# One list, two orders: 3,498 steps of an attention and MLP kernel rearranged around its loads

## The chip, the cores and the metric

One core of a Trainium2 chip. The metric is the device time of one execution in microseconds (us). Five engines work beside each other, each on its own queue of instructions, strictly in order: TensorE (PE, matmuls), VectorE (DVE), ScalarE (ACT), GpSimd (POOL) and SyncE (SP). Here POOL and SP do little but start transfers, which 16 DMA engines then carry out.

## What is computed

Four batches of 6080 tokens with 256 channels. In each batch a 256 x 256 matrix of scores between channels is made from q and k, and v is multiplied by its softmax; a two-layer MLP with 2048 hidden units follows.

```
qn = q / (norm(q, axis=1) + 1e-06);  kn = k / (norm(k, axis=1) + 1e-06)
s  = kn.transpose(0, 2, 1) @ qn / tau
a  = softmax(s, axis=-1)
x  = (v @ a).reshape(B * N, 256)
out = gelu_tanh(x @ w_in) @ w_out
```

## The kernel before

**Tiling.** Since `v @ a @ w_in` is `v @ (a @ w_in)`, the kernel makes one 256 x 2048 matrix `aw` for each batch. The tokens are cut into 25 blocks numbered 0 to 24: five of 1024 and one of 960 in each of the first three batches (blocks 0-5, 6-11, 12-17), and in the last batch five of 1024 (18-22), one of 512 and one of 448. A block runs through the first layer, the GELU, the second layer and the store of its tokens. Both layers use a seven-product scheme in place of eight, with sums made on DVE and copies on ACT. While the blocks of one batch run, the gram matrix, norms and `aw` of the next batch are made in between. Before block 0 there is a start in which batch 0's own q and k are read; the change does not touch it.

**The list.** Everything after that start is one string, `ORDER`, of 3,498 words. `run` takes the words one by one and issues the instructions of each; no scheduler moves them. A word is a step, an optional index, an optional PSUM bank and a block or a batch: `m5.1@b:2` is the fifth small product of set 1 of block 2 into bank b. So the order in which an engine works is the order of the words that issue something on it. Engines are tied to each other by semaphores only, so a word that stands later in the list may still run earlier than its neighbours on another engine.

The words that matter here:

- `lq.c:b`, `lk.c:b` (`load_one`, line 103): POOL starts a load of chunk c of q or k of batch b, 768 rows, cast to bf16 on the way. There are five buffers of each. The load is held back until the latest first- or second-layer product ahead of it in the list has ended (`GATE`).
- `lv.h:n` (`cast_v`, line 442): POOL copies half h of block n of v to a bf16 buffer in DRAM (`vb`), held back in the same way.
- `lt.h:n` (`load_vt`, line 447): SP starts a transposing load from `vb` into `vT`, of which there are two. Nothing holds it back but its data, its buffer, and what stands ahead of it in SP's queue. That is the stores of finished tokens (`store`, line 757), each of which waits for its transposes on DVE.
- `qsq`, `ksq` (`square_op`, lines 158 and 160): the squares of a chunk of q or k, the k of even chunks on DVE and the others on ACT. `row.c_r:b` (line 205): one row group of the chunk into the gram matrix, on PE. These are the uses of a q or k load.
- `vs:n` (lines 558-561, DVE): sums of the transposed halves of v. `g.u:n` (line 482, PE): a plain first-layer product, which reads both halves. `m1` to `m7` (line 482): the small products. These are the uses of `vT`.
- `e.p_t:0` and `E` (block 0's first layer, on PE and ACT), `G`, `wGq`, `wGr`, `wGx` (GELUs on ACT), `wcq`, `wy5` (copies on ACT, lines 613 and 616), `wap`, `wax` (sums on DVE, lines 618 and 621), `T` (sums on DVE, line 704), `M` (second layer, PE), `c11` to `c22` (transposes into the store tile `ot`, DVE, line 744; there are three tiles).
- `D` (second layer of block 24, PE), `sA`, `sB` (its stores).

```
        after(nc.gpsimd.dma_start(out=vb[: y - x, :], in_=v[b, t0 + x : t0 + y, :]), gate)
...
        nc.sync.dma_start_transpose(out=vt_tile(n)[:, :, x:y], in_=v_bf.pop((n, h))[: y - x, :])
...
            elif what in ("lq", "lk"):
                load_one(n, *a, "qk".index(what[1]), GATE[0])
            elif what == "lv":
                cast_v(n, *a, GATE[0])
            elif what == "lt":
                load_vt(n, *a)
```

Of the kernel before, what the change touches and what calls it, by code (L numbers as in the profile page):

```python
# [948 lines left out]
e.0_0@h:0 aw.3@s:0 ac.3:0 aw.2@a:0 e.1_0@b:0 vp.1@r:0 ac.2:0 E.0_0:0 e.2_0@h:0 aw.4@p:0 E.1_0:0  # L949
e.3_0@b:0 lv.1:1 lk.0:1 E.2_0:0 aw.5@s:0 vc.1_0:0 vc.1_1:0 E.3_0:0 e.3_1@h:0 aw.6@a:0 E.3_1:0  # L950
e.0_1@b:0 E.0_1:0 ac.4:0 e.2_1@h:0 ac.5:0 SW.0:0 aw.7@r:0 pA11:0 e.1_1@b:0 E.2_1:0 ac.7:0 e.5_1@h:0
vp.0@p:1 lq.0:1 E.1_1:0 E.5_1:0 e.4_1@b:0 T1.1:0 pF0:0 pS3:0 e.5_0@h:0 pA12:0 vc.0_1:1 ac.6:0
E.4_1:0 M1.0@s:0 pF1:0 vc.0_0:1 e.4_0@b:0 lt.1:1 pS1:0 E.5_0:0 e.6_1@h:0 lq.1:1 pNA:0 E.4_0:0
E.6_1:0 M1.1@s:0 e.6_0@b:0 e.7_1@h:0 ksq.0:1 pS4:0 T1.0:0 lk.1:1 E.6_0:0 row.0_1@r:1 M5.1@a:0
row.0_0@r:1 m1.1@p:1 g.0@b:1 row.0_2@r:1 E.7_1:0 vs:1 lq.2:1 m5.1@h:1 M5.0@a:0 qsq.0:1 wcq.1:1 G.0:1
m6.1:1 f1.0:1 e.7_0@b:0 wy5.1:1 lk.2:1 wap.1:1 m2.1:1 row.0_5@r:1 row.0_4@r:1 row.0_3@r:1 m7.1:1
pA21:0 f2.0:1 SW.1:0 m3.1:1 E.7_0:0 y5:0 wGq.1:1 wax.1:1 g.8@b:1 row.1_4@r:1 T3.0:0 f3.0:1 lv.0:2
row.1_2@r:1 cq:0 m4.1:1 g.10@h:1 wGr.1:1 row.1_3@r:1 row.1_1@r:1 G.8:1 sp.0@p:1 lv.1:2 pS2:0 T2.0:0
T2.1:0 sa.0:1 M2.1:0 M2.0:0 ksq.1:1 qsq.1:1 g.2@b:1 G.10:1 f1.1:1 c11:0 lk.3:1 M6.0:0 f2.1:1
m1.5@p:1 M6.1:0 m5.5@h:1 ap:0 row.1_0@r:1 wcq.5:1 f3.1:1 G.2:1 wy5.5:1 lq.3:1 m2.5:1 m6.5:1  # L960
row.1_5@r:1 T3.1:0 wap.5:1 gc:1 g.3@b:1 M3.1:0 sp.1@r:1 ksq.2:1 lk.4:1 G.3:1 M7.0:0 m3.5:1 M3.0:0
g.11@b:1 T4.0:0 lt.1:2 qsq.2:1 wGq.5:1 lt.0:2 g.12@h:1 f1.2:1 sa.1:1 f2.2:1 M7.1:0 f3.2:1 c12:0
sp.2@r:1 ax:0 wGx.1:1 m7.5:1 G.11:1 m1.6@s:1 sa.2:1 wax.5:1 T4.1:0 G.12:1 g.4@b:1 row.2_1@r:1 lq.4:1
M4.0:0 T1.0:1 m5.6@h:1 row.3_2@r:1 row.3_4@r:1 qsq.3:1 wcq.6:1 G.4:1 m6.6:1 g.7@b:1 wy5.6:1 M4.1:0
wap.6:1 ksq.3:1 lq.5:1 row.3_5@r:1 T2.0:1 wGx.5:1 G.7:1 m4.5:1 m3.6:1 m2.6:1 m7.6:1 row.2_2@r:1
g.15@b:1 f1.3:1 f2.3:1 wax.6:1 wGq.6:1 wGr.5:1 lv.0:3 f3.3:1 c21:0 row.3_0@r:1 row.2_0@r:1 m4.6:1
G.15:1 sp.3@p:1 row.2_5@r:1 row.2_3@r:1 sa.3:1 vs:2 row.2_4@r:1 qsq.4:1 row.3_1@r:1 m1.1@a:2 g.0@h:2
m5.1@b:2 row.3_3@r:1 wcq.1:2 M1.1@p:1 lk.5:1 G.0:2 wy5.1:2 ksq.4:1 m6.1:2 T1.1:1 m2.1:2 wap.1:2
f1.4:1 g.3@h:2 wGx.6:1 wGr.6:1 m3.1:2 m7.1:2 M5.1@s:1 G.3:2 wax.1:2 f2.4:1 lk.6:1 g.8@h:2 f3.4:1
gc:1 wGq.1:2 T2.1:1 m4.1:2 M5.0@s:1 sp.4@r:1 M1.0@p:1 wGx.1:2 lv.1:3 G.8:2 y5:1 m5.2@b:2 sa.4:1  # L970
m1.2@r:2 c22:0 wGr.1:2 T3.0:1 cq:1 m1.5@a:2 m5.5@h:2 wcq.2:2 M2.1:1 m6.2:2 wcq.5:2 M2.0:1 m2.2:2
m6.5:2 wy5.2:2 wy5.5:2 ksq.5:1 T4.1:1 m2.5:2 wap.2:2 c11:1 wap.5:2 m3.2:2 lq.6:1 m7.2:2 wax.2:2
T4.0:1 M6.1:1 M6.0:1 m3.5:2 m4.2:2 wGq.2:2 qsq.5:1 lv.0:4 wGr.2:2 wGq.5:2 g.11@b:2 ap:1 m7.5:2
wGx.2:2 T3.1:1 wax.5:2 f1.5:1 M7.0:1 m1.6@r:2 M7.1:1 m5.6@h:2 G.11:2 lt.0:3 ax:1 f2.5:1 f3.5:1
m4.5:2 g.4@b:2 wcq.6:2 m6.6:2 wGr.5:2 M3.0:1 wy5.6:2 wGx.5:2 sp.5@a:1 M3.1:1 wap.6:2 sa.5:1 G.4:2
m1.7@a:2 m5.7@b:2 m7.6:2 qsq.6:1 ksq.6:1 M4.0:1 m3.6:2 m2.6:2 wcq.7:2 m6.7:2 wy5.7:2 lt.1:3 wax.6:2
m4.6:2 M4.1:1 wGq.6:2 wGx.6:2 f1.6:1 wap.7:2 lq.7:1 m7.7:2 m3.7:2 m2.7:2 f2.6:1 c12:1 g.12@h:2
wax.7:2 wGr.6:2 m1.1@p:3 wGq.7:2 c21:1 T1.0:2 wGx.7:2 row.5_3@r:1 G.12:2 m4.7:2 g.0@b:3 f3.6:1 vs:3
row.5_2@r:1 row.5_0@r:1 row.5_1@r:1 row.5_5@r:1 row.4_2@r:1 row.4_1@r:1 row.5_4@r:1 row.4_4@r:1
m5.1@h:3 wcq.1:3 m1.2@s:3 wGr.7:2 T1.1:2 row.4_3@r:1 G.0:3 sp.6@a:1 m6.1:3 wy5.1:3 m2.1:3  # L980
row.4_5@r:1 wap.1:3 m5.2@b:3 wcq.2:3 lk.7:1 m6.2:3 row.4_0@r:1 sa.6:1 qsq.7:1 m7.1:3 wy5.2:3
M5.1@a:2 m2.2:3 m3.1:3 wax.1:3 gc:1 m4.1:3 M5.0@a:2 wap.2:3 wGx.1:3 wGq.1:3 wGr.1:3 m1.3@r:3 m3.2:3
T3.0:2 m7.2:3 m5.3@h:3 wax.2:3 c22:1 T2.0:2 y5:2 wcq.3:3 wGq.2:3 M1.0@p:2 M1.1@p:2 m6.3:3 wy5.3:3
m4.2:3 T2.1:2 g.8@b:3 m2.3:3 wap.3:3 cq:2 M2.0:2 M2.1:2 ksq.7:1 lv.1:4 wGr.2:3 m3.3:3 m1.5@s:3
M6.0:2 G.8:3 lt.0:4 wGq.3:3 f1.7:1 T3.1:2 f2.7:1 m7.3:3 m5.5@b:3 c11:2 wcq.5:3 f3.7:1 wGx.2:3
g.4@h:3 wy5.5:3 m6.5:3 wax.3:3 wap.5:3 M6.1:2 G.4:3 ap:2 m4.3:3 wGr.3:3 m2.5:3 wGx.3:3 m3.5:3 m7.5:3
wGq.5:3 m5.6@h:3 T4.0:2 sp.7@r:1 M7.1:2 sa.7:1 m1.6@r:3 wcq.6:3 wax.5:3 M7.0:2 m6.6:3 T4.1:2 m4.5:3
wy5.6:3 pow:1 g.12@b:3 wGx.5:3 wap.6:3 wGr.5:3 m2.6:3 m3.6:3 ax:2 G.12:3 kf:1 lt.1:4 lv.0:5 m7.6:3
m1.7@s:3 M4.0:2 wax.6:3 m5.7@b:3 c22:2 wcq.7:3 wGq.6:3 wy5.7:3 m6.7:3 m4.6:3 wGr.6:3 wGx.6:3 wap.7:3
M4.1:2 g.0@h:4 m7.7:3 row.6_2@r:1 m3.7:3 c21:2 m2.7:3 row.7_3@r:1 G.0:4 m1.1@a:4 wax.7:3 m4.7:3  # L990
M3.1:2 M3.0:2 lq.0:2 lv.1:5 wGq.7:3 T1.0:3 vs:4 m5.1@h:4 wGr.7:3 wcq.1:4 c12:2 wy5.1:4 m1.2@s:4
m6.1:4 row.6_5@r:1 m2.1:4 m5.2@b:4 row.7_2@r:1 wap.1:4 wcq.2:4 T1.1:3 m1.3@p:4 row.6_1@r:1 m6.2:4
wGx.7:3 wy5.2:4 wap.2:4 m3.1:4 row.7_1@r:1 m2.2:4 m7.1:4 row.7_5@r:1 wGq.1:4 row.6_4@r:1 wax.1:4
m3.2:4 m7.2:4 row.6_0@r:1 row.7_0@r:1 row.6_3@r:1 row.7_4@r:1 m5.3@h:4 wcq.3:4 T2.1:3 wGq.2:4
wGx.1:4 m4.1:4 m6.3:4 gc:1 m5.4@b:4 m2.3:4 wy5.3:4 wGr.1:4 M5.0@r:3 wax.2:4 wap.3:4 m1.4@a:4 wy5.4:4
m4.2:4 wGx.2:4 lv.0:6 m3.3:4 m7.3:4 M5.1@r:3 T2.0:3 wcq.4:4 wax.3:4 wGr.2:4 m6.4:4 kr:1 lv.1:6
wGq.3:4 lt.0:5 M1.0@s:3 m4.3:4 M1.1@s:3 wGr.3:4 m2.4:4 y5:3 T4.1:3 cq:3 krp@p:1 wap.4:4 wGx.3:4
T4.0:3 m5.5@h:4 m7.4:4 S.1:1 wy5.5:4 th.1:1 S.0:1 th.0:1 wax.4:4 m3.4:4 M2.1:3 m1.5@p:4 T3.0:3
wcq.5:4 M6.0:3 m4.4:4 m6.5:4 M2.0:3 T3.1:3 lt.1:5 wGx.4:4 wGr.4:4 wGq.4:4 wap.5:4 m1.6@a:4 M6.1:3
dn:1 m3.5:4 m7.5:4 m2.5:4 m5.6@b:4 c11:3 wcq.6:4 ap:3 wGq.5:4 wy5.6:4 m6.6:4 wax.5:4 M7.0:3 rc.2:1  # L1000
wap.6:4 m4.5:4 m2.6:4 lk.0:2 g.8@h:4 rc.1:1 wGr.5:4 wGx.5:4 m7.6:4 m3.6:4 m1.7@p:4 M7.1:3 G.8:4
wax.6:4 M3.0:3 m5.7@h:4 m4.6:4 rc.0:1 ax:3 rc.3:1 wGq.6:4 wcq.7:4 c22:3 wGr.6:4 wy5.7:4 M4.0:3
m6.7:4 wap.7:4 M4.1:3 m2.7:4 lv.0:7 wGx.6:4 lq.1:2 m3.7:4 eT:1 m7.7:4 g.0@b:5 c21:3 wax.7:4 wGq.7:4
T1.1:4 G.0:5 rsum@a:1 aw.1@r:1 m4.7:4 g.4@h:5 vs:5 rs:1 M3.1:3 g.8@b:5 c12:3 G.4:5 wGr.7:4 T1.0:4
ac.1:1 m1.1@a:5 m5.1@h:5 aw.0@p:1 wcq.1:5 G.8:5 M5.1@s:4 aw.4@r:1 m6.1:5 wy5.1:5 wGx.7:4 ac.0:1
m2.1:5 m5.2@b:5 m1.2@p:5 wap.1:5 ac.4:1 M5.0@s:4 T2.1:4 m7.1:5 lk.1:2 m3.1:5 lv.1:7 wcq.2:5 y5:4
wy5.2:5 wGq.1:5 wax.1:5 m6.2:5 T3.1:4 M1.1@r:4 m4.1:5 wGr.1:5 M1.0@r:4 m2.2:5 lt.0:6 cq:4 wGx.1:5
wap.2:5 aw.5@a:1 T3.0:4 m7.2:5 g.12@h:5 m3.2:5 T2.0:4 wax.2:5 ac.5:1 wGq.2:5 lt.1:6 M2.1:4 m1.3@a:5
M2.0:4 m4.2:5 m5.3@b:5 wcq.3:5 wy5.3:5 wGx.2:5 wGr.2:5 G.12:5 T4.1:4 m6.3:5 M6.1:4 M6.0:4 c11:4
ksq.0:2 aw.2@p:1 wap.3:5 m7.3:5 m3.3:5 m2.3:5 ap:4 wax.3:5 M7.0:4 m5.5@h:5 ac.2:1 wGq.3:5 m4.3:5  # L1010
m1.5@p:5 M3.0:4 m5.6@b:5 wy5.5:5 wcq.5:5 M3.1:4 m6.5:5 lv.0:8 qsq.0:2 M7.1:4 wGr.3:5 SW.0:1 T4.0:4
c12:4 m1.6@a:5 wap.5:5 aw.3@r:1 ax:4 ac.3:1 wGx.3:5 wcq.6:5 m7.5:5 m3.5:5 m2.5:5 wGq.5:5 M4.0:4
f1.0:2 wy5.6:5 m6.6:5 wax.5:5 wap.6:5 m1.7@r:5 m5.7@h:5 M4.1:4 m2.6:5 m4.5:5 c21:4 m7.6:5 wcq.7:5
m3.6:5 wGx.5:5 wy5.7:5 m6.7:5 wax.6:5 wGr.5:5 aw.6@s:1 wap.7:5 aw.7@p:1 wGq.6:5 m4.6:5 m2.7:5 T1.0:5
m3.7:5 m7.7:5 ac.7:1 wGx.6:5 wGr.6:5 wGq.7:5 g.0@b:6 wax.7:5 ac.6:1 G.0:6 M1.1@a:5 lq.2:2 m1.1@p:6
m4.7:5 lk.2:2 T1.1:5 M5.0@s:5 g.8@h:6 vs:6 lt.0:7 M5.1@s:5 m5.1@b:6 wcq.1:6 wGr.7:5 wGx.7:5 m6.1:6
G.8:6 m1.2@r:6 M1.0@a:5 SW.1:1 wy5.1:6 y5:5 cq:5 lt.1:7 m5.2@h:6 wap.1:6 m2.1:6 m7.1:6 T2.0:5
wax.1:6 m3.1:6 M2.1:5 wcq.2:6 wy5.2:6 m2.2:6 m6.2:6 wGq.1:6 m4.1:6 wap.2:6 M6.0:5 m3.2:6 wGr.1:6
m5.5@b:6 T2.1:5 T3.0:5 m1.5@p:6 M2.0:5 m7.2:6 wGx.1:6 wGq.2:6 wy5.5:6 g.3@h:6 M6.1:5 wcq.5:6 c11:5
# [260 lines left out]
```

## Time and profile before

| | us |
|---|---|
| runs | 687.57, 690.52, 697.32 |
| median of them | 690.52 |
| the profiled execution | 687.86 |
| its span, first to last instruction | 686.1 |
| first matmul of the list begins | 37.91 |
| last matmul ends | 681.03 |
| PE busy | 665.7 (97%) |
| DVE busy | 629.1 (92%) |
| ACT busy | 621.9 (91%) |

A time in the texts that follow is counted from the start of the span of the profiled execution, unless it is a length. "Busy" counts an instruction from its start to its end; PE's ends are modelled and overlap, so the distance between the starts of two matmuls says more than their lengths do. An "idle before" in square brackets is idle time of an engine ahead of an instruction, with what ended it.

### The profile page before, as it was taken

The numbers are of one execution on the slowest core, as the hardware profiler recorded it, in microseconds if no ns is written. First come the engines' busy times: TensorE is split into PE (matmuls) and PEld (weight loads), VectorE is DVE, ScalarE is ACT, GpSimd is POOL, SyncE is SP. The second block draws the span as 40 slices with busy tenths as digits, with TensorE's granted clock in tenths as the row PEclk, the third lists the DMA queues.
The fourth block names the chain that finished last, engine by engine and source line by source line (L and its number), as shares of the span: only waits on it lengthen the run. The fifth ranks groups of instructions, "written<-read, shape, count | busy, mean of one in ns | idle before, by whom it ended". The sixth has DMA issues, their size and how long they took to land.

```text
span 686.1 us, 10286 instructions
## 1 busy us (share of the span) xinstructions
PE 665.7 (97%) x3584; PEld 337.1 (49%) x3584; DVE 629.1 (92%) x938; ACT 621.9 (91%) x941; POOL 74.2 (11%) x137
## 2 busy tenths in 40 slices
PE   3999999999999999999999999989999999999997
PEld 2854445454445454544444545535444444444566
DVE  3579999999999999999999999979999999999994
ACT  5389999998899999999989999979989999999983
POOL 4321111110001010100010101101000000000001
PEclk9999999999999999999999999999999999999999
DMA  9999897584888987655569998636473543445415
GB/s 240 207 251 158 124 171 114 102 143 74 142 103 118 167 114 98 100 96 93 103 105 142 142 157 138 84 53 108 79 135 62 91 75 61 72 83 90 76 32 89
DMA packets 161508, 78.80 MB, mean 115 GB/s; under 512 B 148512, under 2 KB 152224, under 8 KB 160736
## 3 DMA queue, kind: packets, MB, share of 16 engines
q0 software_dynamic: 14480, 39.72, 36.8%
q1 hardware_dynamic: 145728, 37.14, 31.4%
q10 hardware_dynamic: 1248, 1.28, 0.6%
q8 instruction: 28, 0.46, 0.3%
q14 instruction: 24, 0.20, 0.1%
HBM read 78.91 MB, written 36.57 MB: 168 GB/s over the span
## 4 chain that ended last, share of the span: by engine, by line
PE 85%; DMA 7%; issue 4%; ACT 2%; POOL 1%; DVE 0%; DVEq 0%; POOLq 0%; ACTq 0%
PE p L482 22%; PE r L482 17%; PE rb L482 16%; PE qp L482 12%; PE h L482 10%; PE G L205 4%; DMA qk_g1b<-in_k_dram 3%; PE awp L374 2%; DMA qk_g1a<-in_q_dram 1%; DMA k<-in_k_dram 1%; DMA q<-in_q_dram 1%; ACT g L516 1%; PE e L482 1%; ACT g L637 0%; ACT qp L613 0%
## 5 line engine op out<-in xcount | busy, mean ns | idle before, releaser
L482 PEld LDWEIGHTS <-wcomb 128*128 128x128 bf16 x1408 | 136.5, 98 | 144.5 <-issue 1.7
L482 PE MATMUL p<-t,wcomb 128*128 128x512 bf16 (+2 forms) x576 | 142.8, 373 | 0.1
L482 PE MATMUL r<-g,wcomb 128*128 128x512 bf16 (+2 forms) x576 | 141.8, 373 | 0.0
L626 ACT ACTIVATE g<-qp 128x1024 bf16<-128x1024 f32 (+1 forms) x130 | 132.0, 1022 | 6.1 <-PE qp L482 5.9
L482 PEld LDWEIGHTS <-aw 128*128 128x128 bf16 x872 | 84.8, 98 | 94.8 <-issue 6.3
L704 DVE TENSOR_TENSOR t<-g,t 128x2048 bf16<-128x2048 bf16 (+2 forms) x96 | 112.8, 1182 | 0.0
L482 PE MATMUL rb<-tv,sw 128*128 128x512 bf16 (+3 forms) x288 | 101.4, 366 | 0.1
L618 DVE TENSOR_TENSOR qp<-rb,yw 128x512 f32<-128x512 f32 (+2 forms) x137 | 93.1, 686 | 8.7 <-ACT yw L616 4.8
L621 DVE TENSOR_TENSOR xw<-rb,yw 128x512 f32<-128x512 f32 (+2 forms) x137 | 92.6, 676 | 7.1 <-ACT g L637 3.4
L516 ACT ACTIVATE g<-h 128x1024 bf16<-128x1024 f32 (+1 forms) x92 | 94.1, 1032 | 1.8 <-PE h L482 1.4
L482 PE MATMUL h<-vT,aw 128*128 128x512 bf16 (+2 forms) x376 | 95.0, 377 | 0.6 <-ACT g L516 0.5
L616 ACT ACTIVATE yw<-qp 128x512 f32<-128x512 f32 (+2 forms) x137 | 80.8, 601 | 5.8 <-PE qp L482 4.1
L613 ACT ACTIVATE qp<-rb 128x512 f32<-128x512 f32 (+2 forms) x137 | 80.8, 595 | 4.7 <-PE rb L482 3.4
L637 ACT ACTIVATE g<-xw 128x512 bf16<-128x512 f32 (+1 forms) x130 | 82.1, 635 | 2.2 <-DVE xw L621 2.2
L482 PEld LDWEIGHTS <-sw 128*128 128x128 bf16 x576 | 56.2, 98 | 56.6 <-issue 0.6
L637 ACT ACTIVATE g<-rb 128x512 bf16<-128x512 f32 (+1 forms) x130 | 77.6, 602 | 1.9 <-PE rb L482 1.8
L704 DVE TENSOR_TENSOR t<-g 128x2048 bf16<-128x2048 bf16 (+2 forms) x48 | 56.5, 1181 | 0.7 <-ACT g L626 0.4
L704 DVE TENSOR_TENSOR g<-g,g 128x2048 bf16<-128x2048 bf16 (+2 forms) x48 | 56.6, 1183 | 0.0
L442 POOL DMA_DIRECT2D vb<-in_v_dram x45 | 22.5, 501 | 312.1 <-PE rb L482 199.4
L482 PE MATMUL rb<-tv,aw 128*128 128x512 bf16 (+3 forms) x144 | 50.9, 366 | 2.5 <-DVE xw L621 2.5
L482 PE MATMUL rb<-vT,aw 128*128 128x512 bf16 (+3 forms) x144 | 51.3, 366 | 0.0
L482 PE MATMUL qp<-vT,aw 128*128 128x512 bf16 (+3 forms) x144 | 51.3, 366 | 0.0
(143 smaller groups left out, 815.2 us busy)
## 6 DMA issues: line engine op xcount, KB each, us to landing
out_dram<-ot SPq DMA_DIRECT2D x160, 128.0 KB, 3.1
vb<-in_v_dram POOLq DMA_DIRECT2D x38, 256.0 KB, 4.6
k<-in_k_dram POOLq DMA_DIRECT2D x21, 384.0 KB, 5.6
q<-in_q_dram POOLq DMA_DIRECT2D x21, 384.0 KB, 5.2
out_dram<-ot SPq DMA_DIRECT2D x24, 120.0 KB, 4.0
wst<-in_moe_w_out_dram POOLq DMA_DIRECT2D x2, 1024.0 KB, 10.5
vb<-in_v_dram POOLq DMA_DIRECT2D x6, 240.0 KB, 4.1
qk_f<-in_k_dram ACTq DMA_DIRECT2D x2, 512.0 KB, 6.9
```

The costliest lines, as they stand in the source:

```text
L205: nc.tensor.matmul(G[b][:, jc, :], lhsT=qt[:np_, r, jc * 128 : jc * 128 + 128], rhs=kt[:np_, r, :], start=first and jc == 0, stop=jc == 1, ...
L374: nc.tensor.matmul(ps, lhsT=ET[b][:, jc, ic * 128 : ic * 128 + 128], rhs=win_bf[:, jc, fs * 512 : fs * 512 + 512], start=jc == 0, stop=jc ...
L442: after(nc.gpsimd.dma_start(out=vb[: y - x, :], in_=v[b, t0 + x : t0 + y, :]), gate)
L482: GATE[0] = nc.tensor.matmul(*a, skip_group_check=True, **kw)
L516: nc.scalar.activation(g_half(n, u // 8)[:, u % 8].rearrange("p (t x) -> p t x", t=2), hp[:, :, :hc], AF.Gelu_apprx_tanh)
L613: apart(n, i, 0, "act", nc.scalar.activation(QP[n, i][:, 0, :w], RB[n, i][:, :w], AF.Copy))
L616: apart(n, i, 1, "act", nc.scalar.activation(YW[n, i][:, :w], QP[n, i][:, 1, :w], AF.Copy))
L618: apart(n, i, 1, "dve", nc.vector.tensor_add(QP[n, i][:, 1, :w], RB[n, i][:, :w], YW[n, i][:, :w]))
L621: nc.vector.tensor_add(XW[n, i][:, :w], RB[n, i][:, :w], YW.pop((n, i))[:, :w])
L626: nc.scalar.activation(g[:, k0].rearrange("p (t x) -> p t x", t=2), qp[:, :, :hc], AF.Gelu_apprx_tanh)
L637: nc.scalar.activation(g[:, k0, t], x[:, :w], AF.Gelu_apprx_tanh)
L704: nc.vector.tensor_sub(o, a, b)
```

## The change

Only `ORDER` differs. Both lists hold the same 3,498 words, PSUM banks aside: no step is added or removed, and each engine has the same instructions to do. Nearly all of them stand in another place, and many products go to another bank. The rule behind the new order is that transposing loads of v lie apart from loads of q and k, and that the first use of each load lies some us behind its landing. Cut to the places that are spoken of (the left-out lines differ throughout as well):

```diff
-e.0_0@h:0 aw.3@s:0 ac.3:0 aw.2@a:0 e.1_0@b:0 vp.1@r:0 ac.2:0 E.0_0:0 e.2_0@h:0 aw.4@p:0 E.1_0:0
-e.3_0@b:0 lv.1:1 lk.0:1 E.2_0:0 aw.5@s:0 vc.1_0:0 vc.1_1:0 E.3_0:0 e.3_1@h:0 aw.6@a:0 E.3_1:0
-e.0_1@b:0 E.0_1:0 ac.4:0 e.2_1@h:0 ac.5:0 SW.0:0 aw.7@r:0 pA11:0 e.1_1@b:0 E.2_1:0 ac.7:0 e.5_1@h:0
-vp.0@p:1 lq.0:1 E.1_1:0 E.5_1:0 e.4_1@b:0 T1.1:0 pF0:0 pS3:0 e.5_0@h:0 pA12:0 vc.0_1:1 ac.6:0
-E.4_1:0 M1.0@s:0 pF1:0 vc.0_0:1 e.4_0@b:0 lt.1:1 pS1:0 E.5_0:0 e.6_1@h:0 lq.1:1 pNA:0 E.4_0:0
-E.6_1:0 M1.1@s:0 e.6_0@b:0 e.7_1@h:0 ksq.0:1 pS4:0 T1.0:0 lk.1:1 E.6_0:0 row.0_1@r:1 M5.1@a:0
-row.0_0@r:1 m1.1@p:1 g.0@b:1 row.0_2@r:1 E.7_1:0 vs:1 lq.2:1 m5.1@h:1 M5.0@a:0 qsq.0:1 wcq.1:1 G.0:1
...
-m1.5@p:1 M6.1:0 m5.5@h:1 ap:0 row.1_0@r:1 wcq.5:1 f3.1:1 G.2:1 wy5.5:1 lq.3:1 m2.5:1 m6.5:1
...
-m4.6:14 lk.7:3 wGq.7:14 wax.7:14 m1.2@a:15 row.5_4@s:3 T1.0:14 g.0@b:15 m4.7:14 wGr.6:14 G.0:15
...
-m6.2:15 gc:3 wy5.1:15 wy5.2:15 wGx.7:14 wap.1:15 ksq.7:3 M5.1@p:14 m7.1:15 wap.2:15 wax.1:15
...
-m3.3:24 wGq.3:24 wGx.2:24 wGx.1:24 m7.3:24 D.2_1@r:24 D.2_0@s:24 D.6_0@s:24 D.0_0@s:24 c21:23 c22:23
...
-c11:24 c21:24 sB:24 D.4_1@r:24 D.7_1@r:24 D.0_1@r:24 D.3_1@r:24 c22:24 c12:24 sA:24
+e.1_0@h:0 aw.3@s:0 ac.3:0 aw.2@a:0 e.0_0@b:0 ac.2:0 vp.1@r:0 E.1_0:0 vc.1_1:0 vc.1_0:0 e.2_0@h:0
...
+SW.0:0 E.3_1:0 e.2_1@h:0 aw.6@a:0 E.0_1:0 e.1_1@b:0 lv.1:1 E.2_1:0 aw.7@r:0 ac.6:0 ac.7:0 pA11:0
+pA21:0 E.1_1:0 e.5_1@h:0 pF0:0 vp.0@p:1 vc.0_1:1 e.4_0@b:0 E.5_1:0 lq.0:1 pS1:0 T1.0:0 e.4_1@h:0
+M1.1@s:0 E.4_0:0 E.4_1:0 pF1:0 pA12:0 e.6_1@b:0 T1.1:0 vc.0_0:1 ksq.0:1 e.6_0@h:0 lt.1:1 vs:1
+M1.0@s:0 E.6_1:0 E.6_0:0 lq.1:1 e.5_0@b:0 pNA:0 E.5_0:0 e.7_1@h:0 E.7_1:0 M5.0@a:0 lk.1:1 g.0@b:1
+m1.1@r:1 row.0_5@p:1 qsq.0:1 m5.1@h:1 row.0_3@p:1 wcq.1:1 row.0_4@p:1 row.0_0@p:1 lk.2:1 wy5.1:1
...
+G.3:1 M2.0:0 wGr.1:1 m5.5@h:1 sp.0@r:1 M2.1:0 pS2:0 G.10:1 qsq.1:1 ksq.1:1 T2.1:0 sa.0:1 lq.3:1
...
+G.2:1 wGx.1:1 f3.1:1 M7.0:0 sp.1@p:1 wap.5:1 m3.5:1 g.11@b:1 lv.1:2 qsq.2:1 T3.1:0 ksq.2:1 M7.1:0
+M3.0:0 G.11:1 wGq.5:1 lk.4:1 f1.2:1 ax:0 f2.2:1 sa.1:1 f3.2:1 g.4@b:1 g.12@h:1 sp.2@p:1 T4.0:0 G.4:1
+M3.1:0 G.12:1 sa.2:1 m7.5:1 T4.1:0 M4.0:0 m1.6@p:1 g.7@b:1 wax.5:1 m5.6@h:1 c12:0 lt.1:2 lt.0:2
...
+vs:2 g.0@h:2 row.3_5@s:1 row.2_3@s:1 m1.1@r:2 wGr.6:1 lq.5:1 g.3@b:2 sp.3@p:1 G.0:2 row.3_0@s:1
...
+m4.5:14 g.4@b:14 lk.7:3 wGx.5:14 wcq.6:14 wGr.5:14 m6.6:14 f3.5:3 wy5.6:14 G.4:14 M3.0:13 sp.5@r:3
...
+m1.5@s:15 wap.3:15 c11:14 M6.1:14 m5.5@b:15 m2.3:15 wcq.5:15 ap:14 ksq.7:3 m7.3:15 m3.3:15 m6.5:15
...
+m4.2:24 m7.3:24 D.4_1@r:24 m3.3:24 wGr.2:24 c21:23 wGx.2:24 wGq.2:24 wax.3:24 c22:23 D.5_0@p:24
...
+c11:24 sB:24 c12:24 c22:24 sA:24
```

## The prediction

> **What bounds the kernel now.** First the page: busy shares, the span in slices and the granted clock.
>
> ```profile
> span 686.1 us, 10286 instructions
> ## 1 busy us (share of the span) xinstructions
> PE 665.7 (97%) x3584; PEld 337.1 (49%) x3584; DVE 629.1 (92%) x938; ACT 621.9 (91%) x941; POOL 74.2 (11%) x137
> ...
> PE   3999999999999999999999999989999999999997
> ...
> PEclk9999999999999999999999999999999999999999
> ```
>
> PE is busy everywhere but in the first slice and once past the middle, and the clock never falls. As PE's ends are modelled, I read its pace from starts, in the timeline of PE:
>
> ```profile
> 44.84 1.89 PE L482 MATMUL e<-vT,aw 128*128 128x512 bf16 x8
> 46.57 0.59 PE L374 MATMUL awp<-win_bf,eT 128*128 128x512 bf16 x2
> ```
>
> Eight matmuls of 512 columns take 46.57 - 44.84 = 1.73 us, 0.216 us each; other widths go by their columns. At that pace the list's matmuls come to 637.3 us. They begin at 37.91 and end at 681.03, which is 643.1 us. So all waiting of PE inside the list is 643.1 - 637.3 = 5.8 us, and no order of the same matmuls can win more there. The waits of PE name the large ones:
>
> ```profile
> PE G L205 <- ACT qk_g1a L131: 9.9, 2, 7.0
> PE rb L482 <- DVE xw L621: 2.5, 1, 2.5
> PE ss L257 <- DVE a L243: 1.3, 1, 1.3
> PE h L482 <- ACT g L516: 0.5, 1, 0.5
> ```
>
> The first and third lie before the list. The other two I follow back: the chain of waits, then the timelines of SP, ACT and PE around 440 us.
>
> ```profile
> 439.30 9.03 DMA k<-in_k_dram
> ```
> ```profile
> 438.94 1.47 SPq L447 DMA_TRANSPOSE vT<-vb  x1
> ```
> ```profile
> 448.36 1.58 ACT L158 ACTIVATE sq<-k 128x1280 bf16<-128x1280 bf16 x2 [2.90 <-DMA k<-in_k_dram]
> ```
> ```profile
> 451.23 0.38 PE L482 MATMUL rb<-tv,aw 128*128 128x512 bf16 x1 [2.49 <-DVE xw L621]
> ```
>
> The load `lk.7:3` is issued 0.36 us behind a transposing load and needs 9.03 us; from 44 us on the median of the k loads is 5.8 and the smallest 4.1. ACT stands 2.90 us at its square, `wGx` behind it comes late, DVE's sum waits for the register tile that it frees, and PE waits 2.49 us. The same in small at 71 us: `lq.3:1`, between two transposing loads (69.86 and 71.13), needs 7.71 us on the chain, its square goes late on ACT, and PE waits at 81.78 for a GELU. The views of the tiles `vT`, k and q from 44 us on give landings of 3.1/5.3/12.4, 4.1/5.8/12.4 and 3.8/4.9/9.9 us (least, median, most). By single issues in the trace, 18 of the 45 transposing loads take over 7 us. A q or k load issued 0.3 to 1.8 us behind a transposing one takes 5.4 to 12.4 us; with none in flight, 30 take 4.9 at the median.
>
> **The change, part by part.** The instructions of every engine are the same, so there are only waits to price. I place a word by the PE work ahead of it, in us from the list's begin, and add 37.91 and the waits so far. Check: `rsum:3` has 454.8 us ahead of it, so 492.7; it ran at 497.70, so 5.0 of the 5.8 us of waiting lie before it.
>
> *The wait at 451.* `lk.7:3` has 5.8 us of PE work between issue and square before, and 21.8 after, with no transposing load within 5 us. Gone: 2.66 us by the distance of starts there, and 0.27 at the next gap. 2.9 us. What would be late next is nothing of its kind: the nearest of the q and k loads to its use in the new list, `lq.0:1`, has 8.0 us (before: 5.8, 6.8, 6.9, 6.9, 7.0, 7.0), and only 3 of 48 have less than 10 (before 12). Hidden work, if a collision comes all the same: 8 us cover the median, 12.4 would show 4.4.
>
> *The waits at 81.8 and 85.1.* By starts 0.67 and 0.26. `lq.3:1` gets 14.3 us in place of 9.7. 0.9 us.
>
> *Block 1's v, new.* `lv.1:1` moves from 5.2 to 9.5 us of PE work, `g.0@b:1`, the first reader of both halves, from 19.7 to 19.0. Before:
>
> ```profile
> 43.57 0.54 POOL L442 DMA_DIRECT2D vb<-in_v_dram  x1 [5.49 <-PE e L482]
> ```
> ```profile
> 49.97 23.35 SPq L447 DMA_TRANSPOSE vT<-vb  x3
> ```
>
> POOL issued 0.46 us behind 37.91 + 5.2, the copy took 6.38 us, and the transposing load 5.00. After: issue at 37.91 + 9.5 + 0.46 = 47.9. The copy takes between 3.5 (the least of v's) and 6.4, I take 4.4, as `lk.0` now goes ahead of it; SP issues at 52.3. The transposing load takes between 3.1 and 12.4 us; I take 5.0, since its nearest row is that same load, with a q load issued 0.75 us ahead of it as `lq.0` is here by 1.8. It lands at 57.3, and `g.0@b:1` is due at 37.91 + 19.0 = 56.9. PE waits 0.4 us (0 to 9.8 with both worst). Queued behind it on PE are `m1` and row groups; on DVE `vs:1` now stands ahead of `f1` and `wap.1`. DVE's own work up to `vs:1`, with its waits for the `aw` products, ends at about 56.4, so DVE waits 0.9 us, of which PE sees little beyond its own 0.4. I take 0.5.
>
> *Block 2's v, new.* `lv.1:2` moves from 27.1 to 35.7; issue 74.5 with 0.5 us of waits so far, copy 4.5, two transposing loads from 79.0 and 80.4. Two alone took 3.8 and 3.4 us, or 3.9 and 5.4 (336.0, 312.8), so the second lands at 84 to 86. Due: `g.0@h:2` at 37.91 + 47.2 + 0.5 = 85.6. 0.3 us; up to 5 with 10 us beside the loads `lk.4` and `lv.0:3`. From block 3 on at least 12 us of PE work lie between the earliest issue of a `vT` and its use.
>
> *The end.* The last two transposes wait for a store tile:
>
> ```profile
> 681.65 0.72 DVE L744 STREAM_TRANSPOSE ot<-o 128x224 f32<-128x224 f32 x2 [1.40 <-DMA out_dram<-ot]
> ```
>
> PE ends at 681.03, so 0.5 us can go. `c21:23`, which starts the store that frees the tile, now stands 5.7 us of PE work ahead of the end and not 4.0. I take 0.5 (0 to 0.6).
>
> *All else.* The other small waits, 5.8 - 3.9 = 1.9 us, may be others in the new list. Evidence for no new bound: per 40 us of PE work, DVE has at most 40.7 us and ACT 41.3 at their own pace of starts (before 40.1 and 40.7), and the shortest distance from `m1` to `m6`, across a copy on ACT, is 0.82 us against 0.86. I take 0, with both ends below.
>
> Sum: 687.86 - 2.9 - 0.9 + 0.5 + 0.3 - 0.5 = 684.4 us, against the profiled execution. That one lies 2.7 us below the median of the runs (690.52) and by the fastest of them (687.57).
>
> **The rivals.** *The loads are not parted on the chip.* No product holds a transposing load back; it goes when `vb`, buffer and SP's stores let it, up to 15 us of PE work ahead of its word. Against it: worked out that way, one q or k load of the new list falls 0 to 4 us behind a transposing one, some fifteen of the old. If it holds, the 3.8 us stay: 684.4 + 3.8 = 688.2.
>
> The Trainium skill (DMA: Bandwidth & Descriptors, Rules for kernel authors) says that a transpose next to ordinary DMAs needs nothing. That sentence is about wrong data, but read as a rule for time it would have the parting bring 0 and the time come out as in this rival. The 9.03 us beside a transposing load, against 4.9 with none in flight, speak against reading it so.
>
> *Slower: block 1's transposing load is hit.* It flies between `lq.0` (50.5) and `lq.1` (54.8). With 12.4 us it lands at 64.7, and PE waits 7.8 us: 684.4 - 0.4 + 7.8 = 691.8. It decides when the load lands later than 60.8, where the wait eats the 3.5 us of the other terms. For it: two of the transposing loads with a q or k load behind them took 12.2 to 12.4. Against: 5.00 with both neighbours in the old list.
>
> *Slower: many small waits.* PE has next to no slack, and all its words moved. One wait of 0.3 us, as the old list had at 118.4, in each of the 22 seven-product blocks 1 to 22 adds 6.6: 691.0; at 0.67 each it is 699. For it: ACT's 41.3 in 40. Against: the old list, as tight by the same counts, had 1.9 us in all.
>
> **How the numbers follow.** My forecast 0.60 (its own range 681.6, all 5.8 and 0.5 us gone, to 687), loads not parted 0.16, block 1 hit 0.08, small waits 0.13, several at once 0.03. The range for 8 in 10 is 681.5 to 693: all of the forecast and the first rival, and the rivals of 691 to 692. A measurement of this kernel can tell about 2% from no change, that is below 676.7 or above 704.3. The first is out of reach by the 5.8 us; I leave 0.01. The second needs 16 us more than the other cases give: the 0.03 and a little of the small waits, 0.05. Within 2%: 0.94.
>
> **What would show it.** Right: PE waits for nothing over 1 us in the list; no q or k load over 8 us; ACT never waits for k from 440 to 450; the last transposes begin within 0.2 us of PE's end. Block 1: PE waits at its first `h` product from 56.9 us on, for a transposing load. Wrong: transposing loads that start within 2 us of a q or k load and last 9 to 12 us; or a PE whose starts show more than 3 us of gaps that no load ends.

## The result, and the profile after

The changed kernel takes 685.63 us (median of 17 runs, 685.07 to 686.70). Beside it the kernel before took 690.07 (17 runs, 687.57 to 697.32). The ratio is 0.9924, with a 95% interval of 0.9906 to 0.9941: 4.4 us faster by the medians, and much steadier, as its runs lie within 1.6 us of each other and those of before within 9.8. The profiled execution took 685.17 us (before 687.86).

The page of the changed kernel, its span, its busy times and PE's row of slices:

```profile
span 683.4 us, 10285 instructions
## 1 busy us (share of the span) xinstructions
PE 665.6 (97%) x3585; PEld 337.1 (49%) x3585; DVE 628.5 (92%) x938; ACT 621.7 (91%) x941; POOL 74.1 (11%) x137
...
PE   3999999999999999999999999999999999999997
...
PEclk9999999999999999999999999999999999999999
```

No busy share has changed; the one 8 in PE's row has gone. (The one matmul more fills 32 columns of a bank and takes 0.03 us; products that moved to another bank brought it.) By starts of matmuls the list now runs from 38.15 to 678.12 us, 640.0 long. Against the 637.3 us of its matmuls, the prediction's figure, that leaves 2.7 us of waiting (before 5.7 in the same reading). The waits of PE, longest first:

```profile
PE G L205 <- ACT qk_g1a L131: 6.8, 1, 6.8
PE G L205 <- DVE qk_g1a L133: 2.6, 1, 2.6
PE ss L257 <- DVE a L243: 1.0, 1, 1.0
PE G L205 <- DMA qk_g1b<-in_k_dram: 0.9, 1, 0.9
PE e L482 <- DVE aw L416: 0.8, 1, 0.8
PE rb L482 <- ACT qp L613: 0.3, 1, 0.3
PE rb L482 <- DVE qp L618: 0.2, 1, 0.2
```

The first five belong to the start and to block 0's first product. The last two are copies on ACT and sums on DVE: inside the list no wait of PE goes back to a load any more. The place where PE stood 2.66 us is quiet: in ACT's timeline the square of `lk.7:3` has no idle time ahead of it.

```profile
451.76 0.58 ACT L613 ACTIVATE qp<-rb 128x512 f32<-128x512 f32 x1 [0.21 <-PE rb L482]
452.26 1.56 ACT L158 ACTIVATE sq<-k 128x1280 bf16<-128x1280 bf16 x2
```

The view of `vT` from 44 us on says that the loads are parted on the chip too (least, median, most, where 12.4 was the most before). By single issues 1 of 45 transposing loads takes over 7 us (18 before) and 2 of 54 loads of q and k (11 before).

```profile
DMA to landing us min/median/max: 3.2/4.3/7.5
```

Block 1's v, which the prediction watched, in the timelines of POOL, SP, DVE and PE:

```profile
48.33 0.54 POOL L442 DMA_DIRECT2D vb<-in_v_dram  x1 [2.92 <-PE e L482]
```
```profile
52.66 1.34 SPq L447 DMA_TRANSPOSE vT<-vb  x1
```
```profile
56.99 0.69 DVE L558 TENSOR_TENSOR tv<-vT 128x1024 bf16<-128x1024 bf16 x1
```
```profile
57.55 1.03 PE L482 MATMUL h<-vT,aw 128*128 128x512 bf16 x4
```

The transposing load landed at 56.9, DVE's sum and PE's product followed, and neither has idle time in brackets.

### The profile page after: what moved, and what is told of

Same layout as the page of the kernel before. It is cut to its first block, busy times and chain, and to the rows that moved or that the text cites. A ratio compares the mean times of both kernels' runs of the same rounds, so it can differ in the third digit from the quotient of the medians.

```text
span 683.4 us, 10285 instructions
## 1 busy us (share of the span) xinstructions
PE 665.6 (97%) x3585; PEld 337.1 (49%) x3585; DVE 628.5 (92%) x938; ACT 621.7 (91%) x941; POOL 74.1 (11%) x137
## 4 chain that ended last, share of the span: by engine, by line
PE 94%; DMA 4%; DVE 0%; ACT 0%; issue 0%; POOL 0%; DVEq 0%; ACTq 0%; POOLq 0%
PE p L482 24%; PE r L482 18%; PE rb L482 17%; PE qp L482 13%; PE h L482 12%; PE G L205 5%; DMA qk_g1b<-in_k_dram 3%; PE e L482 2%; PE awp L374 2%; DMA qk_g1a<-in_q_dram 1%; PE o L482 1%; PE ss L186 0%; PE ss L263 0%; ACT qp L613 0%; PE rk L317 0%
## 5 line engine op out<-in xcount | busy, mean ns | idle before, releaser
L482 PE MATMUL qp<-vT,sw 128*128 128x512 bf16 (+3 forms) x144 | 51.4, 366 | 0.0
## 6 DMA issues: line engine op xcount, KB each, us to landing
wst<-in_moe_w_out_dram POOLq DMA_DIRECT2D x2, 1024.0 KB, 11.2
```

The source lines that it names most:

```text
L482: GATE[0] = nc.tensor.matmul(*a, skip_group_check=True, **kw)
```

## The experiments

All are the same instructions in another order of words, but for the last one. Each was timed in five rounds beside the kernel before, and not in the rounds of the changed kernel; a ratio always goes by the kernel before of its own rounds. "Distance" is the PE work, in us, between a load's word and its first use.

### One load alone

```diff
-m4.6:14 lk.7:3 wGq.7:14
+wGq.5:14 lq.7:3 lk.7:3 M7.0:13
```

> The order before, with one word moved: lk.7:3 stands straight behind lq.7:3, 7.9 us of PE work earlier, so that it lands ahead of the transposing load at 439. Theory A (the gain comes from where the loads stand): the wait of PE near 451 goes and nothing takes its place; a profile of about 687.9 - 2.9 = 685.0 us, and about 0.995 to 0.997 of the time before if other executions of the old order stall there as well. Theory B (the gain comes from the new order of products, sums and GELUs, and the stall at 451 would only be paid elsewhere): 1.000, 687 to 690 us.

686.32 us (683.78 to 689.39), ratio 0.9946 [0.9922, 0.9970]. One word of the list of before, moved 7.9 us earlier, takes 4.1 us off the median of its rounds (690.43). The profiled execution, 685.16 us, is what theory A's sum gave (685.0). But the runs still spread over 5.6 us, and ACT still waits at the other place, for `lq.3:1`, which takes 8.3 us:

```profile
ACT sq L158 <- DMA q<-in_q_dram: 1.3, 1, 1.3
```

### Load words alone, and steps alone

Two hybrids. The first keeps the old steps and puts all load words (`lq`, `lk`, `lv`, `lt`) where the new list has them, by PE work ahead of them. The second has the new steps and the load words at their old places.

```diff
 (old steps)
-lq.c:b lk.c:b lv.h:n lt.h:n at the old list's PE work
+lq.c:b lk.c:b lv.h:n lt.h:n at the new list's PE work
```

> The steps in the order before, but every word that starts a load or a transposing load stands at the place of the new list, counted in PE work. Theory A (loads): nearly all of the gain, 0.992 to 0.995 of the time before, 685 to 687 us, runs within 2 us of each other as with the new list. Theory B (steps): about the time before, 0.998 to 1.002, runs spread over several us.

> The reverse: the steps in the new order, the loads and transposing loads at the places of the old list. Theory A (loads): about the time before, 0.998 to 1.005, 688 to 692 us, with q and k loads of 9 to 12 us beside transposing loads in its profile. Theory B (steps): nearly all of the gain, 0.992 to 0.995.

Load words alone: 685.71 us (685.22 to 688.12), 0.9945 [0.9922, 0.9968]. Steps alone: 690.10 us (686.64 to 692.49), 0.9982 [0.9957, 1.0007], no difference that the interval can tell from none. So the gain is in where the loads stand, and the other words bring none by themselves. The second hybrid is no clean opposite, though. Among the new steps `lk.7:3` has 14.8 us to its use, it takes 4.3 us, and PE doesn't stand at 451 in the profile, of the fastest execution (686.64 us). What keeps the median at 690.10 no profile shows; `lq.3:1` still has only 10 us here, and took 8.3. The new steps fit the loads a little: with the loads alone, DVE and PE wait for block 2's `vT`,

```profile
DVE tv L558 <- DMA vT<-vb: 1.4, 1, 1.4
```

which the whole change has not.

### Distance without parting

The old list, with the fifteen q and k loads that had less than 14 us of distance moved ahead to 14 or more. The transposing loads stay where they are.

```diff
-lk.0:1 at 5.2, lq.0:1 at 11.3, lq.1:1 at 15.6, lk.1:1 at 18.2, ... lk.7:3 at 398.7
+lk.0:1 at 3.9, lq.0:1 at 3.9, lq.1:1 at 10.8, lk.1:1 at 10.8, ... lk.7:3 at 389.8
```

> The order before, with the 15 loads of q and k that had under 14 us of PE work up to their first use moved earlier, to 14 us and more; where transposing loads stand is not looked at. Theory A1 (the distance to the use is what counts, a slow landing then costs nothing): 0.992 to 0.996, 685 to 687 us, with transposing loads still beside q and k loads and landings of 9 to 12 us in the profile. Theory A2 (the parting counts): collisions hit other uses, 0.997 to 1.002.

683.90 us (683.86 to 684.16), 0.9908 [0.9879, 0.9938]: better than expected, in the median 1.7 us below the changed kernel, and within 0.3 us from run to run. In its profile 13 q and k loads take over 7 us, the longest 12.6, and 11 transposing loads, the longest 12.4 (11 and 18 in the list of before). From 44 us on PE waits for none of them; one wait for a load is left on DVE. `lq.3:1` is one of the slow ones: it takes 8.9 us beside the same two transposing loads as before, with 14.7 us to its use, and nobody waits. `lk.7:3` is not: it now goes out clear of transposing loads and takes 5.6 us, so for this word the run doesn't hold distance and parting apart.

```profile
DVE tv L558 <- DMA vT<-vb: 1.0, 1, 1.0
```

### Parting without distance

The new list, with 45 q and k loads moved later, each to a place clear of transposing loads; 25 of them then have 6.8 to 7.5 us.

```diff
-lk.0:1 at 6.1, lq.1:1 at 16.4, lk.1:1 at 19.0, lq.3:1 at 28.2, ...
+lk.0:1 at 7.4, lq.1:1 at 21.4, lk.1:1 at 21.4, lq.3:1 at 33.6, ...
```

> The new list with 45 q and k loads moved later, each to a place where no transposing load of the new list's profile is in flight, so that 25 of the 48 words have 6.8 to 7.5 us of PE work up to their first use, as the six shortest of the old list had (5.8 to 7.0). Parting without distance. If parting is enough (landings of 4 to 5.5 us): as the new list, 685 to 687 us, 0.991 to 0.995 of the time before. If distance is what counts: some loads still land late in some executions, 686 to 691 us, runs spread over 3 us and more, 0.995 to 1.002.

702.23 us (699.01 to 704.26), 1.0185 [1.0144, 1.0226]: slower than the kernel before, and than either expectation. The transposing loads stay short (3 of 45 over 7 us, the longest 7.4), but 12 q and k loads take over 7 us, and many now go out 0.5 us behind each other: of three issued at 424.66, 425.18 and 425.70 us the first took 5.8, the second 7.1 and the third 9.9 us. The load of k issued at 125.22 takes 6.9 us with 7.0 to its use, ACT stands 2.82 us at its square, and PE 2.95. The copy of block 2's v is slower too (7.2 us, 3.9 in the changed kernel), so PE waits for that `vT`. The waits of ACT and PE, from 44 us on:

```profile
ACT sq L158 <- DMA k<-in_k_dram: 7.2, 3, 4.1
```
```profile
PE rb L482 <- DVE qp L618: 4.3, 4, 2.8
PE qp L482 <- ACT g L516: 2.8, 1, 2.8
PE h L482 <- DMA vT<-vb: 2.2, 2, 1.9
```

Of the change's two rules, distance brings the whole gain, though many loads still collide. What parting is worth alone stays open: here it was bought with distance (25 loads under 8 us, where the old list has 6) and with collisions of another kind, and a list that parts the loads and keeps the old distances was not run. For one load the run does show it: `lq.3:1` has 8.7 us here, less than before (9.7), lands after 4.3, and its square on ACT has no wait.

### One load put back

The new list with `lk.7:3` 16 us later, behind block 16's transposing loads, 5.6 us ahead of its use.

```diff
-m4.5:14 g.4@b:14 lk.7:3 wGx.5:14
+M1.0@r:14 lk.7:3 T2.0:14
```

> The new list with one word moved: lk.7:3 stands 16 us of PE work later, 5.6 us ahead of its first use and right behind the transposing loads of block 16, as in the old list. The reverse of the run with that one word moved earlier. Theory A (loads): the wait of PE near 451 is back, 2 to 5 us, and the runs spread; 687 to 691 us, 0.996 to 1.000. Theory B (steps): 685 to 686.5 us, 0.992 to 0.994.

686.76 us (686.12 to 687.59), 0.9961 [0.9941, 0.9981]. The list is 1.6 us longer than the changed kernel's, and the old wait is back, but smaller than expected: the load takes 6.2 us and not 9.0, PE loses 1.3 us and not 2 to 5, and the runs stay within 1.5 us of each other. ACT's timeline:

```profile
454.11 1.58 ACT L158 ACTIVATE sq<-k 128x1280 bf16<-128x1280 bf16 x2 [1.81 <-DMA k<-in_k_dram]
```

### More distance in the new list

The new list's eleven loads with less than 14 us, moved ahead to 14 or more.

```diff
-lk.0:1 at 6.1, lq.0:1 at 12.1, lq.1:1 at 16.4, lk.1:1 at 19.0, ...
+lk.0:1 at 0.0, lq.0:1 at 6.1, lq.1:1 at 13.9, lk.1:1 at 13.9, ...
```

> The new list with the 11 loads that had under 14 us of PE work up to their use moved earlier, to 14 us and more. The old list gained 6.5 us by that and went to 683.9. If the new list waits for no load already: 685 to 686, 0.992 to 0.994, and its 1.7 us over the old list with early loads are due to its steps. If load waits are left in it: 683.5 to 684.5, 0.990 to 0.991.

689.84 us (686.93 to 691.19), 1.0000 [0.9975, 1.0024]: the whole gain gone, against both expectations. What the prediction feared for block 1's v happens here. The loads of q and k issued at 52.67 and 53.22 us now meet block 1's transposing load, issued at 53.32, which takes 8.3 us in place of 4.2. PE's timeline:

```profile
57.39 0.38 PE L482 MATMUL h<-vT,aw 128*128 128x512 bf16 x1
61.65 1.01 PE L482 MATMUL h<-vT,aw 128*128 128x512 bf16 x2 [3.88 <-DMA vT<-vb]
62.46 0.63 PE L482 MATMUL rb<-vT,aw 128*128 128x512 bf16 x1
62.88 0.42 PE L205 MATMUL G<-k,q 128*128 128x256 bf16 x1
```

By starts PE loses 4.05 us there, yet the list is 6.2 us longer than the changed kernel's. The windows of four us around the wait show the rest. The first five numbers behind each stretch's length are busy times (PE, PEld, DVE, ACT, POOL), then come the granted clock, the DMA's share and its GB/s:

```profile
54.00:58.00 4.00, 3.77 (x18) 1.70 (x18) 2.88 (x4) 4.00 (x6) 0.00 (x0) 1.00 1.02 176
58.00:62.00 4.00, 0.35 (x1) 0.10 (x1) 0.30 (x1) 1.48 (x2) 0.00 (x0) 0.84 0.46 86
62.00:66.00 4.00, 4.00 (x15) 2.04 (x14) 2.36 (x5) 2.09 (x3) 0.58 (x2) 0.50 0.17 21
66.00:70.00 4.00, 4.00 (x19) 1.79 (x18) 3.77 (x6) 2.40 (x3) 0.47 (x1) 0.81 0.98 168
70.00:74.00 4.00, 3.95 (x24) 1.93 (x24) 3.96 (x9) 4.00 (x6) 0.98 (x2) 1.00 0.44 75
```

The clock falls to 0.50 at 60.71 us, inside the wait, and stays there until 67.53. In the timeline the matmul of 512 columns at 62.46 has 0.42 us to the next start, where the pace of the list is 0.216. So the wait is paid, and then some 2 us more.

### The same, with block 1's v ahead as well

```diff
-lv.1:1 at 9.5
+lv.1:1 at 5.2
```

> The new list with its eleven short-distance q and k loads moved ahead to 14 us or more before use, as in the run that gave 689.84 and in whose profile the only wait of PE for a load was 4.05 us for block 1's vT; here block 1's load of v is also moved ahead of the load of q of block 0, by 5.2 us of PE's work. Theory that block 1's v is all that was lost there: its transposing load starts about 5 us sooner and the wait goes; with it goes the low granted clock behind the wait (0.50 from 62 to 66 us in that profile); 684 to 686 us, 0.991 to 0.993 of before. Rival, that the early loads hurt the list in other places too (pools, POOL's queue): 688 to 690, 0.997 to 1.000, with other waits in the list.

685.07 us (684.76 to 685.46), 0.9915 [0.9887, 0.9943]. One word moved 4.3 us earlier (the expectation's 5.2 is its new place) takes back 4.8 us, PE waits for no load again, and the list is 640.0 long, as the changed kernel's. So that collision was all that was lost, and the added distance of the eleven others brings nothing that can be told (685.07 beside 685.63).

### The kernel before, once more

> The kernel before once more, for a second profile of it and a test of the comparison by itself. Theory A: a ratio of 0.998 to 1.002; the profile shows waits of PE of 3 to 9 us in the list, all behind loads with under 10 us to their use, and not the same ones as in the first profile (there 2.66 at 451 and 0.93 near 82): the landings differ from run to run, which spreads the times over 687 to 697. Against it: the same two waits with the same lengths again.

690.82 us (687.43 to 692.96), 1.0009 [0.9985, 1.0033]. Its second profile, of 691.82 us, has its large waits at the same two places, against what theory A says of the places, but not with the same lengths. The load of q at 70.6 us, `lq.3:1`, took 11.1 us here, 7.7 in the first profile:

```profile
81.88 1.48 ACT L158 ACTIVATE sq<-q 128x1536 bf16<-128x1536 bf16 x1 [4.07 <-DMA q<-in_q_dram]
```

Gaps of PE's starts are 4.1 us around 82 and 2.6 at 455, 6.7 in all, where the first profile had 3.9. Here too the granted clock falls behind the waits:

```profile
78.00:82.00 4.00, 2.43 (x14) 1.08 (x13) 3.30 (x5) 0.12 (x1) 0.53 (x1) 1.00 1.22 86
82.00:86.00 4.00, 1.97 (x8) 0.73 (x7) 0.70 (x2) 4.00 (x5) 0.00 (x0) 0.86 1.05 206
86.00:90.00 4.00, 3.95 (x16) 1.81 (x16) 2.81 (x4) 2.76 (x4) 0.53 (x1) 0.71 0.02 4
90.00:94.00 4.00, 4.00 (x30) 2.54 (x30) 3.84 (x9) 4.00 (x6) 0.50 (x1) 1.00 1.11 164
```

The list is 4.4 us longer than in the first profile: 2.8 by the gaps, and 1.2 by the lost 29% of the four us from 86, with something of the 14% ahead of them.

### Two loads alone

The list of before, with `lk.7:3` at 13.7 us of distance (from 5.8) and `lq.3:1` at 14.7 (from 9.7).

```diff
-m4.6:14 lk.7:3 wGq.7:14
+wGq.5:14 lq.7:3 lk.7:3 M7.0:13
...
-wy5.5:1 lq.3:1 m2.5:1
+T2.1:0 sa.0:1 lq.3:1 M2.1:0
```

> The list of before with two words moved and nothing else: block 7's fourth load of k to 13.7 us ahead of its first use (from 5.8), block 3's second load of q to 14.7 us (from 9.7). Theory that these two loads are the whole of what the change mended: 683.8 to 685.5 us, 0.990 to 0.993, times within 2 us of each other, no wait of PE for a load of q or k over 0.5 us in the profile. Rival, that the others with 9 to 14 us matter as well, or that moving the first load only hands its collision on: 686 to 687 as with the k load alone (686.32), spread of some 5 us, with a wait of 0.5 to 2 us somewhere else.

683.86 us (683.68 to 684.16), 0.9898 [0.9870, 0.9926]. The two words are `lk.7:3`, chunk 7 of k of batch 3, and `lq.3:1`, chunk 3 of q of batch 1; the expectation calls the numbers blocks. They bring the whole gain: as fast as fifteen moved loads, and steady. The median lies 1.8 us below the changed kernel's, though the intervals of the two ratios overlap. The waits of PE behind the start:

```profile
PE e L482 <- DVE aw L416: 0.4, 1, 0.4
PE rb L482 <- DVE sv L193: 0.2, 1, 0.2
```

Single transfers in the traces show what each word did to its neighbours (us from issue to landing):

| | before | second profile of before | two loads moved |
|---|---|---|---|
| near 70: transposing loads | 8.7, 8.4 | 11.9, 11.9 | 5.0, 4.6 |
| `lq.3:1` | 7.7 | 11.1 | 5.6 |
| load of k at 73 | 7.8 | 11.2 | 5.9 |
| near 440: transposing load | 9.8 | 9.4 | 3.5 |
| `lk.7:3`, its two transfers | 9.0, 8.8 | 8.7, 8.3 | 5.7, 5.4 |

At these two places the moved word parts the transfers as well, so this run can't tell distance from parting. For `lq.3:1` either is enough: with fifteen loads moved it was slow, far from its use, and free, and in the run of parting without distance near, quick, and free. For `lk.7:3` no run holds the two apart.

The other loads of this list show that a short distance alone costs nothing either. Ten still have under 10 us, five of them 6.8 to 7.0; those five land after 3.7 to 4.5 us, the ten after 6.8 at most, and nobody waits. It takes both, a near use and a slow landing.

The runs also say which of the two words makes the times uneven. Where `lq.3:1` stands near its use, beside transposing loads, the times lie 5.5 us or more apart: the kernel before, `lk.7:3` moved alone, steps alone. With `lk.7:3` put back alone they lie 1.5 apart.

### The end

The list with fifteen loads moved, and the stores of the last block but one spread over two engines (line 748).

```diff
-(nc.sync, nc.sync, nc.gpsimd, nc.gpsimd)
+(nc.sync, nc.scalar, nc.sync, nc.scalar)
```

> The list of before with fifteen loads of q and k moved early (683.90 us), and the stores of the last block given to the engines in the order sync, scalar, sync, scalar in place of sync, sync, gpsimd, gpsimd. Theory that SP's wait of 1.4 us for its last two stores is what kept the changed kernel's end at 5.3 us behind PE's last matmul: 0.5 to 1.0 us less, 683.0 to 683.4 us, PE's end to the span's end 4.3 to 4.8 us. Rival, that the end is set by how long the last store takes to land, whoever issues it: 683.7 to 684.1, the end at 5.2 to 5.4 us.

683.83 us (683.60 to 684.07), 0.9897 [0.9867, 0.9928], against 683.90 without it: no gain. DVE no longer waits for a store tile, but the stretch from PE's end to the span's end stays at 5.2 us, and SP's queue, in its last 10 us, waits for earlier stores more than with the old stores (1.4 us):

```profile
SPq L757 <- DMA out_dram<-ot: 3.3, 2, 1.9
```

The theory was that SP's wait goes with the store tile's. The store tile's went, SP's grew. What binds SP's last stores stays open.

## Why the prediction was right, and where not

The forecast was 684.4 us, the timed median 685.63, inside the range of 681.5 to 693 and inside the likeliest case's own. The sum was made against a profiled execution; that of the changed kernel took 685.17. The two large terms were right in mechanism and size, the small ones were not, and some of their misses cancel. Point by point:

- **The wait at 451, -2.9: right.** The gap has gone, moving this one load alone brings 0.9946, and putting it back costs the list 1.6 us (the load was then less slow, 6.2 us).
- **The waits at 81.8 and 85.1, -0.9: right for the profiled execution.** They are gone. In the second profile of before they are 4.1 us, with a low clock behind them: for a slower execution the term is far too small.
- **Block 1's v, +0.5: not paid.** Issue at 48.33 (47.9 forecast), the copy 4.3 us (4.4), the transposing load 4.2 (5.0). It landed at 56.9, 0.4 us sooner than forecast, and the product came at 57.55 without a wait.
- **Block 2's v, +0.3: not paid.** Its transposing loads were issued at 79.1 and 80.4 and landed at 84.3 and 85.1, ahead of the 85.6 at which the product was due.
- **The end, -0.5: failed.** DVE's wait of 1.40 us for a store tile did go,

```profile
678.33 0.71 DVE L744 STREAM_TRANSPOSE ot<-o 128x224 f32<-128x224 f32 x2 [0.44 <-PE o L482]
```

 and still from PE's end to the span's end it is 5.3 us (5.2 before). In SP's queue, over its last 10 us, stands

```profile
SPq L757 <- DMA out_dram<-ot: 1.4, 1, 1.4
```

 and by single issues its four last stores go out at 677.92, 678.28, 680.17 and 680.53 us: two in time, two 1.4 us late. The same wait of 1.4 us stood in SP's queue before the change. The step read the end from DVE and did not follow the queue behind it.
- **All else, 0: nearly.** The list ran 3.0 us shorter, as its terms say (-2.9 - 0.9 + 0.5 + 0.3), but with the 0.8 of the v's unpaid and as much spent in small waits, the largest 0.47 and 0.40 us, behind a copy on ACT and a sum on DVE. That the two cancel is luck. The list began 0.24 us later, in a start that the change does not touch.

So in the profiles the sum missed by 0.8 us, 0.6 by the end and 0.2 by the start. The timed gain is larger than the profiled one (4.4 us by the medians against 2.7) because the execution of before that was profiled lies 2.2 us below the median. The sum inherited that: it is a gain by what this execution lost, and not by what the median one loses. The prediction named the distance, 2.7 us by the runs it had, and did not ask where it sits. The second profile, of 691.82 us, shows it: in the same waits, longer, and in the clock behind them. An execution in the middle of the runs was not profiled, so how the median's loss divides between the two places is open; that the spread stays when `lk.7:3` alone is mended points to `lq.3:1`.

**The rivals.** "Not parted on the chip" is out: 1 transposing load over 7 us. "Block 1's load is hit" did not come with this change, but was a real danger: with `lq.1:1` and `lk.1:1` 2.5 and 5.1 us earlier in the list, it is hit, and the gain is gone. "Many small waits" cost 0.8 us more than was counted, not 6.6.

**The reason behind the forecast** needs a correction. The prediction gave the parting and the distance equal weight. The sentence of the Trainium skill that it weighed (DMA: Bandwidth & Descriptors, Rules for kernel authors: a transpose next to ordinary DMAs needs nothing) gives no price, and the traces show one, up to 12 us for a transfer of 4 to 5. But that price costs nothing where the use is 14 us away: 13 slow loads, no wait of PE. Two loads were both slow and near, and moving these two brings the whole gain.

**What stays open.** The changed kernel is 1.8 us behind the two moved words, by medians of different rounds. In the profiles its list is 0.7 us longer and begins 0.8 us later. In six profiles with the new steps the list begins at 37.84 to 38.15 us, in seven with the old ones at 37.37 to 37.96. Whether the new order of the first words or the chance of the start does that was not tried.

## What to carry to other kernels

When a kernel is bound by one engine that hardly waits, list the loads by their distance to the first use and by the longest landing of their kind, and move those that fall short of it. One that lands quickly needs no move, as ten loads of the list with two moved words show, but which load will be hit changes with the order. Two words brought all that a new order of 3,498 brought here. A load that is moved meets other transfers: look up what has little distance at its new place, as block 1's v had. And look at the spread of the runs before the sum is made: where it is wide, the waits of one profile are one draw of them.

## What the runs showed of the hardware

**A collision slows both sides.** In the kernel before, the 11 q and k loads issued up to 2 us behind a transposing load take 5.4 to 12.4 us, 8.8 at the median; the 29 that meet none take 3.8 to 7.4, 4.8 at the median. The 20 transposing loads with a q or k load issued within 2 us take 3.5 to 12.4 us, 9.1 at the median; the 23 that meet none take 3.1 to 8.1, 3.8 at the median. That the one slows the other shows where a word was moved away: 8.7 and 8.4 us become 5.0 and 4.6 (table above). Loads of q and k on each other's heels land later as well: of three issued 0.5 us apart in the run of parting without distance the last took 9.9 us.

**A wait of PE can cost more than its length.** Behind the wait of 2.66 us in the first profile of before, the granted clock stays at 1.00. Behind waits of 2.95 and 3.00 us in the run of parting without distance, two windows of four us each show 0.78 and 0.79, or 0.79 and 0.79, which is 3.4 us at half clock. Around the 4.05 us it is 0.84, 0.50, 0.81, which is 6.8 us at half clock. The Trainium skill (TensorE: Matmul & The Clock Gate, What's actually happening) has the clock halved after an idle window of about 3.4 us and given back after a busy one. The 3.4 and 6.8 us at half clock agree with one and two such windows; the idle time does not, as waits of 2.95 us were enough. Nor need it be one wait: in the second profile of before no single gap was over 1.73 us, PE was busy for 1.97 of the four us from 82, and 3.4 us at half clock followed.

The traces say more closely what decides. In each, the clock changes only at whole multiples of 3.413 us from its first change. Cut into windows on that grid, with PE's idle time read from the starts, the four windows that end in a fall hold 2.6, 2.7, 2.8 and 3.1 us of it; of the others at full clock none holds more than 2.3. The wait of 2.66 us lay across an edge, 0.9 us in one window and 2.0 with the next gap in the other. So in these runs standing costs extra when 2.6 us of it fall into one window, in one piece or in three; 2.3 us were not enough.
